# Attention in bursts of three units throughout, and the last output columns stored in small groups from two queues

## The chip, the core and the metric

The kernel runs on one core of one Trainium2 chip. The metric is device time in microseconds (us), the median of several executions. A profile shows one execution; its span (first to last instruction) is some 2 us shorter than the device time. PE is the matrix engine (TensorE), DVE is VectorE, ACT is ScalarE, POOL is GpSimd, SP is the engine that only issues transfers.

## The reference, cut to what matters

```python
# q, k, v: (8 batches, 12 heads, 448, 64); d_model 768, d_ff 2048
scores = (q @ k.T) / sqrt(64)
attn   = max(scores, 0)**2 / 448          # no softmax
x      = attn @ v                         # to (3584, 768)
h      = x @ w_in                         # FFN1
g      = max(h, 0) + alpha * min(h, 0)
out    = g @ w_out                        # FFN2, float32
```

## The kernel before

Four heads form a quad; there are three quads to a batch, 24 in all. One **unit** (n, j) is the scores of quad n for one of seven blocks of rows: four matmuls that each use a quarter of PE's array (64x64), side by side. ACT and DVE turn a unit into squares. "av" is the product of a quad's squares with v, 28 quarter matmuls. FFN1 (`hps`) and FFN2 (`ops`) use the full array, 128x128. The program interleaves them by hand: while PE works on the FFN of batch b, bursts of attention units of batch b + 1 are put in between, so that ACT and DVE have time for them.

```python
def scores(n, j, relu="act", space=sc_ps):
    # 4 matmuls into sc_ps (two buffers in all) or into two of the four mm_ps buffers;
    # relu "act": ACT alone, 896 columns; "both": ACT and DVE one half each;
    # "act2": ACT, in two halves; "dve": DVE alone
...
def burst(n, i):                   # batch 1's attention (quads 3 to 5)
    if i == 0:
        scores(n, 0); squares()
        if (n - 1, 0) in att: attnv(n - 1)
    else:
        for j in (2 * i - 1, 2 * i):          # two units
            scores(n, j, ...); squares()
...
play([(3, 3), o[0], turn(4), o[1], (4, 0), o[2], (4, 1), o[3], ...])   # o[i]: 8 FFN2 matmuls
...
def ffn2(sb, c, hf, half):         # 128 rows x 384 columns, 16 matmuls in two steps
    ...
    nc.vector.tensor_copy(o[:, bass.ts(hf, 384)], ps)
    if hf == 1:
        for u in range(2):         # two stores of 64 x 768 float32, both from SP
            nc.sync.dma_start(out=rows[j], in_=o[64 * u:64 * u + 64])
```

From batch 2's attention on, bursts hold three units already; the first takes its buffers from `mm_ps`, the two others from `sc_ps`.

In the views below, `sc` and `sch` are scores in `sc_ps` and in `mm_ps`, `tps` PE's transposes of q and k, `rl` the relus, `at` the squares, and `neg` and `gT` the two steps of FFN1's activation. In the code, `f[i]` and `o[i]` are pieces of FFN1 and FFN2, `turn(n)` is the transposes of quad n, `feed` is casts, and `g("40", "41", "3a")` is a burst of units (4, 0) and (4, 1) with quad 3's av.

## Time and profile before

| | before |
|---|---|
| device time, median | 401.09 us (400.79 to 401.98, 4 runs) |
| span of the profiled run | 399.3 us |
| PE busy | 387.3 us, 97% |
| DVE, ACT, POOL busy | 65%, 55%, 18% |

I cut every profile into five stages by PE's own work, because single stages repeat far better than whole executions of one kernel, which differ by a us or more: with the same instructions, batch 1 and last FFN (below) agree to 0.02 us in all profiles. The **opening** runs from the start of the span to the first FFN1 matmul behind quad 3's transposes. **Batch 1** goes from there to the end of quad 5's av. The **middle** goes on to the first matmul of the last batch's FFN1 (a block of 96). **Last FFN** ends with the last matmul, and the **end** is what is left of the span. Each border is the start or the end of a piece in the chain of work. Before, these are 37.01, 41.92, 276.55, 38.97 and 4.85 us.

### The profile page before, as it was taken

The page shows a single profiled execution, that of the slowest core. Times are in us where ns is not written, and L with a number is a line of the kernel's source. Part 1 is how long each engine was busy: PE and PEld are TensorE (multiplying, and loading weights), DVE is VectorE, ACT ScalarE, POOL GpSimd, SP SyncE. Part 2 cuts the span into 40 slices and gives each one's busy share as a digit, 9 for nine tenths or more (in the row PEclk, how much of TensorE's full clock was granted, in tenths as well). Part 3 has the DMA queues.
Part 4 walks back from the last instruction along what each step waited for, and adds up shares of the span by engine and source line. Part 5 has one row for each costly group of instructions (what it writes and reads, how often), then busy time and mean ns, then how long its engine had stood idle before and what let it go on. Part 6 is the DMA issues. An engine that isn't in the chain of part 4 may idle for free.

```text
span 399.3 us, 7923 instructions
## 1 busy us (share of the span) xinstructions
PE 387.3 (97%) x3201; PEld 200.8 (50%) x3201; DVE 258.1 (65%) x411; ACT 221.0 (55%) x345; POOL 72.8 (18%) x88
## 2 busy tenths in 40 slices
PE   8788999999999999999999999999999999999995
PEld 5434455444555445544555455554555445555562
DVE  3775767768664877567665777768575776736411
ACT  5785754788544766456544775656464585624200
POOL 6564000022021430033020360033002300000000
PEclk9699999999999999999999999999999999999999
DMA  6999995494098933393097961295058720130033
GB/s 145 189 209 205 203 250 204 116 242 150 21 244 202 252 136 80 86 270 100 2 215 197 250 192 43 64 274 155 2 144 187 200 48 0 41 79 2 0 80 79
DMA packets 64164, 55.44 MB, mean 139 GB/s; under 512 B 35696, under 2 KB 59776, under 8 KB 64128
## 3 DMA queue, kind: packets, MB, share of 16 engines
q1 hardware_dynamic: 53152, 44.98, 43.7%
q0 software_dynamic: 10976, 9.96, 15.6%
q8 instruction: 25, 0.41, 0.4%
q14 instruction: 11, 0.09, 0.1%
HBM read 45.62 MB, written 11.01 MB: 142 GB/s over the span
## 4 chain that ended last, share of the span: by engine, by line
PE 92%; DVE 2%; DMA 2%; ACT 1%; issue 1%; POOL 0%; ACTq 0%
PE ops L247 38%; PE hps L231 35%; PE av L202 7%; PE sc L159 6%; PE sch L159 4%; DMA qe<-in_q_dram 2%; DVE at L184 1%; PE tps L134 1%; DMA qraw<-in_q_dram 1%; PE avh L202 1%; ACT rl L173 0%; DVE gT L239 0%; ACT xT L211 0%; ACT xT L217 0%; POOL ke L103 0%
## 5 line engine op out<-in xcount | busy, mean ns | idle before, releaser
L247 PE MATMUL ops<-w_out_sb,gT 128*128 128x384 bf16 x896 | 153.4, 327 | 0.0
L231 PE MATMUL hps<-xT,w_in_sb 128*128 128x448 bf16 x768 | 151.2, 353 | 1.4 <-ACT xT L211 0.5
L184 DVE TENSOR_TENSOR at<-rl 128x896 bf16<-128x896 bf16 x167 | 111.1, 685 | 19.0 <-ACT rl L173 8.8
L247 PEld LDWEIGHTS <-gT 128*128 128x128 bf16 x896 | 84.1, 98 | 67.2 <-issue 14.7
L231 PEld LDWEIGHTS <-w_in_sb 128*128 128x128 bf16 x768 | 73.1, 98 | 75.7 <-issue 10.2
L239 DVE SCALAR_TENSOR_TENSOR gT<-neg,beta_sb,hps 128x448 bf16<-128x448 f32 x128 | 83.9, 677 | 35.7 <-ACT neg L238 35.1
L173 ACT ACTIVATE rl<-sc 128x896 bf16<-128x896 f32 x109 | 95.8, 927 | 7.7 <-PE sc L159 5.3
L238 ACT ACTIVATE neg<-hps 128x448 f32<-128x448 f32 x128 | 68.4, 553 | 55.0 <-PE hps L231 52.9
L255 DVE COPY osb<-ops 128x384 f32<-128x384 f32 x56 | 31.1, 555 | 54.5 <-PE ops L247 54.5
L109 POOL CAST kb<-kraw 128x896 bf16<-128x896 f32 x16 | 16.2, 1011 | 210.0 <-DMA kraw<-in_k_dram 210.0
L165 ACT ACTIVATE rl<-sch 128x448 bf16<-128x448 f32 x37 | 20.1, 544 | 56.4 <-PE sch L159 56.4
L159 PE MATMUL sc<-qT,kT 64*64 64x448 bf16 x464 | 36.4, 362 | 2.7 <-ACT rl L173 2.2
L202 PE MATMUL av<-at,vb 64*64 64x448 bf16 x616 | 33.1, 350 | 0.0
L166 DVE TENSOR_SCALAR rl<-sch 128x448 bf16<-128x448 f32 x37 | 23.0, 620 | 14.1 <-PE sch L159 14.1
L159 PEld LDWEIGHTS <-kT 64*64 64x64 bf16 x672 | 14.9, 106 | 29.6 <-issue 25.0
L202 PEld LDWEIGHTS <-vb 64*64 64x64 bf16 x672 | 20.3, 110 | 13.2 <-issue 1.4
L169 ACT ACTIVATE rl<-sch 128x448 bf16<-128x448 f32 x30 | 14.6, 544 | 16.9 <-PE sch L159 16.9
L217 ACT ACTIVATE xT<-av 128x896 bf16<-128x896 f32 x21 | 19.4, 922 | 6.8 <-PE av L202 6.7
L159 PE MATMUL sch<-qT,kT 64*64 64x448 bf16 x208 | 20.3, 380 | 0.0
L109 POOL CAST qb<-qraw 128x896 bf16<-128x896 f32 x16 | 18.4, 1151 | 0.0
L109 POOL CAST vb<-vraw 128x896 bf16<-128x896 f32 x16 | 16.8, 1053 | 1.4 <-DMA vraw<-in_v_dram 0.8
L171 DVE TENSOR_SCALAR rl<-sc 128x896 bf16<-128x896 f32 x6 | 6.5, 1084 | 2.9 <-PE sc L159 2.9
(47 smaller groups left out, 72.6 us busy)
## 6 DMA issues: line engine op xcount, KB each, us to landing
out_dram<-osb SPq DMA_DIRECT2D x56, 192.0 KB, 2.8
qraw<-in_q_dram SPq DMA_DIRECT2D x19, 448.0 KB, 4.6
kraw<-in_k_dram SPq DMA_DIRECT2D x19, 448.0 KB, 5.3
vraw<-in_v_dram SPq DMA_DIRECT2D x18, 448.0 KB, 6.3
w_out_sb<-in_moe_w_out_dram POOLq DMA_DIRECT2D x2, 1536.0 KB, 19.8
w_in_sb<-in_moe_w_in_dram POOLq DMA_DIRECT2D x8, 192.0 KB, 8.2
w_in_sb<-in_moe_w_in_dram POOLq DMA_DIRECT2D x4, 384.0 KB, 9.7
vb<-in_v_dram POOLq DMA_DIRECT2D x6, 224.0 KB, 9.9
```

What stands on the lines that cost most here:

```text
L109: eng.tensor_copy(o, i)
L159: nc.tensor.matmul(half[r][64 * c:64 * c + 64, :S], kT[n][64 * r:64 * r + 64, j, c, :], qT[n][64 * r:64 * r + 64, :, c, :], start=True, st ...
L165: nc.scalar.activation(rl[:, 0], half[0][:, :S], ACTF.Relu)
L166: nc.vector.tensor_scalar(rl[:, 1], half[1][:, :S], 0.0, None, ALU.max)
L173: nc.scalar.activation(rl, ps[:, :, :S], ACTF.Relu)
L184: nc.vector.tensor_tensor(a, rl, rl, ALU.mult)
L202: nc.tensor.matmul(half[r][64 * s:64 * s + 64, :S], vb[n][64 * r:64 * r + 64, s, j, :], a[64 * r:64 * r + 64, s], start=(j == 0), stop=(j ...
L231: nc.tensor.matmul(ps, w_in_sb[:, km // 2, km % 2, bass.ts(ff, 128)], xT[b][:, km // 2, km % 2, :], start=(km == 0), stop=(km == KM - 1))
L238: nc.scalar.activation(neg, ps, ACTF.Relu, scale=-1.0)
L239: nc.vector.scalar_tensor_tensor(gT[b // 2][:, ff, (b % 2) * S:(b % 2) * S + S], neg, beta_sb[:, ff:ff + 1], ps, ALU.mult, ALU.add)
L247: nc.tensor.matmul(ps, gT[sb][:, ff, bass.ts(c, 128)], w_out_sb[:, ff, bass.ts(hf, 384)], start=(ff == 0), stop=(ff == KF - 1))
L255: nc.vector.tensor_copy(o[:, bass.ts(hf, 384)], ps)
```

## The change

The intent was to have fewer switches between attention and FFN on PE in batch 1's attention, to relieve ACT there, and to shorten what follows the last matmul.

```diff
-def burst(n, i): ...                       # one, two, two, two units of a quad
+def group(units, how="both"): ...          # up to three units or av; the first of three in mm_ps
 ...
-play([..., (3, 0), f[8], f[9], f[10], (3, 1), f[11], f[12], f[13], (3, 2), f[14], f[15]])
+play([..., f[8], g("30", "31", "32"), f[9], f[10], f[11], f[12],
+      g("33", "34", "35"), f[13], f[14], f[15]])
-play([(3, 3), o[0], turn(4), o[1], (4, 0), o[2], (4, 1), o[3], (4, 2), o[4], (4, 3), o[5], o[6], turn(5), o[7],
-      (5, 0), feed(6, "k"), o[8], (5, 1), feed(6, "q"), o[9], (5, 2), feed(6, "v"), o[10], (5, 3), feed(7, "k", "q"), o[11]])
+play([g("36"), turn(4), o[0], o[1], g("40", "41", "3a"), o[2], o[3], g("42", "43", "44"), o[4], o[5],
+      g("45", "46"), o[6], turn(5), o[7], g("50", "51", "4a"), feed(6, "k", "q"), o[8], o[9],
+      g("52", "53", "54"), feed(6, "v"), o[10], g("55", "56"), feed(7, "k", "q"), o[11]])
 ...
-                to_bf16(n, w, nc.scalar)                              # casts of quads 6 and 7
+                to_bf16(n, w, nc.scalar if n == 6 else nc.vector)
 ...
-        n_in, n_out = ((2, 6) if b % 2 else (3, 5))                  # bursts in FFN1, FFN2
-        if b == 1:
-            n_in += 1
+        n_in, n_out = ((2, 7 if b == 1 else 6) if b % 2 else (3, 5))
 ...
+def ffn2_last(sb, c):                      # the last 128 rows only
+    for w in (384, 256, 128):
+        ... 16 matmuls of w columns, then
+        nc.vector.tensor_copy(o[:, lo:lo + w], ps)
+        for u in range(2):
+            (nc.sync, nc.scalar)[u].dma_start(out=rows[j][:, lo:lo + w], in_=o[64 * u:64 * u + 64, lo:lo + w])
```

Quad 8's casts stay on POOL but are issued as an item of their own in batch 1's FFN1.

More of the change, by code (lines that the diff above doesn't have):

```diff
@@ L261, in ffn2 @@
                 nc.sync.dma_start(out=rows[j], in_=o[64 * u:64 * u + 64])
+    def ffn2_last(sb, c):
+        o = o_sb[(sb, c)] = o_pool.tile([128, d_model], F32, tag="o", name="osb")
+        lo = 0
+        for w in (384, 256, 128):
+            ps = mm_ps.tile([128, 384], F32, tag="mm", name="ops")[:, :w]
+            for ff in range(KF):
+                nc.tensor.matmul(ps, gT[sb][:, ff, bass.ts(c, 128)], w_out_sb[:, ff, lo:lo + w],
+                                 start=(ff == 0), stop=(ff == KF - 1))
+            nc.vector.tensor_copy(o[:, lo:lo + w], ps)
+            for u in range(2):
+                blk = 2 * c + u
+                b, j = 2 * sb + blk // NJ, blk % NJ
+                rows = out[b * S:(b + 1) * S].rearrange("(pp j) d -> j pp d", j=NJ)
+                (nc.sync, nc.scalar)[u].dma_start(out=rows[j][:, lo:lo + w], in_=o[64 * u:64 * u + 64, lo:lo + w])
+            lo += w
     def steps(b, what):
@@ L270, with group, f, spread @@
     NQ = len(quads)
-    relu_on_dve = {(n, j) for n in range(NG + 1, 2 * NG) for j in (1, 3, 5)}
-    def burst(n, i):
-        if i == 0:
-            if n < NQ:
-                scores(n, 0)
-                squares()
-            if (n - 1, 0) in att:
-                attnv(n - 1)
-        elif n < NQ:
-            for j in (2 * i - 1, 2 * i):
-                scores(n, j, "dve" if (n, j) in relu_on_dve else "act")
-                squares()
-    def spread(seq, bursts, share=0.92):
+    def group(units, how="both"):
+        def f():
+            order = sorted(units, key=lambda u: u[1] == "av")
+            for i, (n, j) in enumerate(order):
+                if j == "av":
+                    attnv(n)
+                elif i == 0 and len(order) == 3:
+                    scores(n, j, how, mm_ps)
+                else:
+                    scores(n, j)
+            squares()
+            for n, j in order:
+                if n < n_pe:
+                    continue
+                if j == 0:
+                    if n + 2 < NQ:
+                        load(n + 2)
+                    if n + 1 < NQ:
+                        transpose(n + 1, "k")
+                        transpose(n + 1, "q")
+                if j == 4 and n > 2 * NG and n + 2 < NQ:
+                    for w in "kqv":
+                        to_bf16(n + 2, w, nc.gpsimd)
+        return f
+    def spread(seq, items, share=0.92):
         total = sum(x[0] for x in seq) * share
@@ L289, in spread @@
         for cost, fn in seq:
-            while n < len(bursts) and done >= total * n / len(bursts):
-                for f in bursts[n] if isinstance(bursts[n], list) else [bursts[n]]:
-                    f() if callable(f) else burst(*f)
+            while n < len(items) and done >= total * n / len(items):
+                items[n]()
                 n += 1
@@ L295, in spread @@
             done += cost
-        assert n == len(bursts)
+        assert n == len(items)
     warm_w = singles.tile([128, 128], BF16)
@@ L377, in play, with g @@
         for x in seq:
-            if isinstance(x, list):
-                play(x)
-            elif callable(x):
-                x()
-            else:
-                burst(*x)
+            x()
+    def g(*units):
+        return group([(int(u[0]), "av" if u[1:] == "a" else int(u[1:])) for u in units])
     for ff in range(4):
@@ L388 @@
     f = [fn for _, fn in steps(0, "in")]
-    play([f[4], f[5], turn(3), f[6], f[7], (3, 0), f[8], f[9], f[10], (3, 1), f[11], f[12], f[13], (3, 2), f[14], f[15]])
+    play([f[4], f[5], turn(3), f[6], f[7], f[8], g("30", "31", "32"), f[9], f[10], f[11], f[12],
+          g("33", "34", "35"), f[13], f[14], f[15]])
     load_bf16(5)
@@ L412 @@
     stream.append((NQ - 1, "av"))
-    parts, todo_u = [], list(stream)
-    while todo_u:
-        m = 2 if not parts else 3
-        parts.append(todo_u[:m])
-        del todo_u[:m]
-    def group(units, phase):
-        def f():
-            units_ = sorted(units, key=lambda u: u[1] == "av")
-            for i, (n, j) in enumerate(units_):
-                if j == "av":
-                    attnv(n)
-                elif i == 0 and len(units_) == 3:
-                    scores(n, j, "act2" if phase == "in" else "both", mm_ps)
-                else:
-                    scores(n, j)
-            squares()
-            for n, j in units_:
-                if j == 0:
-                    if n + 2 < NQ:
-                        load(n + 2)
-                    if n + 1 < NQ:
-                        transpose(n + 1, "k")
-                        transpose(n + 1, "q")
-                if j == 4 and n + 2 < NQ:
-                    for w in "kqv":
-                        to_bf16(n + 2, w, nc.gpsimd)
-        return f
+    parts = [stream[:2]] + [stream[i:i + 3] for i in range(2, len(stream), 3)]
     count = 0
     for b in range(1, B - 1):
-        n_in, n_out = ((2, 6) if b % 2 else (3, 5))
-        if b == 1:
-            n_in += 1
+        n_in, n_out = ((2, 7 if b == 1 else 6) if b % 2 else (3, 5))
         if b == B - 2:
@@ L450 @@
         mlp = steps(b, "in")
-        spread(mlp[3:] if b == 1 else mlp, [group(x, "in") for x in parts[count:count + n_in]], 0.95)
+        bursts = [group(x, "act2") for x in parts[count:count + n_in]]
+        if b == 1:
+            bursts.append(lambda: [to_bf16(2 * NG + 2, w, nc.gpsimd) for w in "kqv"])
+        spread(mlp[3:] if b == 1 else mlp, bursts, 0.95)
         count += n_in
-        spread(steps(b, "out"), [group(x, "out") for x in parts[count:count + n_out]], 0.92)
+        spread(steps(b, "out"), [group(x) for x in parts[count:count + n_out]], 0.92)
         count += n_out
-    for _, fn in steps(B - 1, "in") + steps(B - 1, "out"):
+    for _, fn in steps(B - 1, "in") + steps(B - 1, "out")[:-4]:
         fn()
+    ffn2_last(B // 2 - 1, NJ - 1)
 _INS = ['q', 'k', 'v', 'moe_w_in', 'moe_w_out', 'moe_alpha']
```

## The prediction

> **What bounds the kernel now.** I read the page's busy shares first, then the chain that ended last, then the list of what TensorE (PE) waited for, then the chain in order of time through batch 1's attention (36 to 79 us) and the timeline of the last 5 us.
>
> ```profile
> PE 387.3 (97%) x3201; PEld 200.8 (50%) x3201; DVE 258.1 (65%) x411; ACT 221.0 (55%) x345; POOL 72.8 (18%) x88
> PE 92%; DVE 2%; DMA 2%; ACT 1%; issue 1%; POOL 0%; ACTq 0%
> ```
>
> PE is busy for 97% of the 399.3 us span and carries 92% of the chain. VectorE at 65% and ScalarE at 55% are far from a bound on average. The list of waits of PE, asked for from 50 us to the end, holds one line:
>
> ```profile
> PE hps L231 <- ACT xT L217: 0.2, 1, 0.2
> ```
>
> So after the opening nothing keeps PE waiting for long. The time can fall only if PE has less to do, or if the 4.8 us after its last matmul get shorter. The stretch that the change rewrites looks so in the chain in order of time (start, duration, what):
>
> ```profile
> 57.37 0.50 PE sc L159 x8
> 57.87 1.41 PE ops L247 x8
> 59.28 0.50 PE sc L159 x8
> 59.78 1.41 PE ops L247 x8
> 61.19 0.31 PE sc L159 x4
> 61.54 0.38 PE sc L159 x4
> 61.92 2.71 PE ops L247 x16
> 64.63 0.90 PE tps L134 x28
> ...
> 104.01 0.31 PE sch L159 x4
> 104.32 0.38 PE sc L159 x8
> 104.70 2.71 PE ops L247 x16
> ```
>
> Attention matmuls here are 64x64 pieces, four side by side; FFN matmuls are 128x128. Eight FFN2 matmuls take 1.41 us and sixteen take 2.71, so one costs (2.71 - 1.41) / 8 = 0.1625 us and each stretch begins with 1.41 - 8 x 0.1625 = 0.11 us extra. One unit of scores (4 matmuls) takes 0.31 us alone, two take 0.50 and three 0.31 + 0.38 = 0.69: 0.19 us for a unit and 0.12 us extra at the start. **An excursion from the full array to small tiles and back costs 0.12 + 0.11 = 0.23 us, whether it carries one unit or three.** From 104 us on bursts already hold three units; in batch 1's attention they hold two. There is also a hole at 61.50 to 61.54 plus a slow first piece: the two units of that burst take 0.73 us instead of 0.50. The burst at 73.80 does the same.
>
> The end of the kernel, from the timeline:
>
> ```profile
> 394.48 0.56 DVE L255 COPY osb<-ops 128x384 f32<-128x384 f32 x1 [2.04 <-PE ops L247]
> 395.06 1.11 SPq L261 DMA_DIRECT2D out_dram<-osb  x2
> ```
>
> After the last matmul (394.45) come one copy of 384 columns, then two stores of 192 KB, issued one after the other from one queue. The second starts 0.55 us after the first. The issue list gives 2.8 us from issue to landing, and the span ends at 399.3.
>
> **What the Trainium skill says.** TensorEngine Tiling, Key Properties: changing the tiling mode, and not only the tile, drains the array. The trace agrees: the extra 0.11 to 0.12 us appears only where small and full tiles meet, and not between scores and attention-times-v, which share a mode (28 of those take 1.32 us right behind scores). TensorE: Matmul & The Clock Gate, Back-to-back issue gap: in a stream of weight load and matmul pairs, 128 columns take about 81 ns, more than the 56 ns of the columns alone. No such stream of full tiles runs in the kernel before, so this prices the new last group. DMA: Bandwidth & Descriptors, Anatomy of one DMA: about 2.0 us fixed, plus bytes at 436 GB/s. For a 192 KB store that gives 2.45 us; the trace has 2.8, with 2.6 the least. The same page, Issuing engines are not separate DMA queues: starting transfers from two engines saves only the time to initiate them, which is the 0.55 us here.
>
> **The change part by part.**
>
> *Batch 1's bursts.* From the instruction order of both kernels, PE's excursions from the start of the first transposes (36.1 us) to the end of quad 5's attention-times-v (78.95) fall from 16 to 12: quad 3's scores 0 to 5 go in two bursts instead of three; quads 4 and 5 lose one burst each; and score 6 of quad 3 stands directly before quad 4's transposes. There a switch from 64x64 to 128x64 tiles remains, about 0.12 us. Saved: 4 x 0.23 - 0.12 = 0.80 us. To check the model: content of this stretch is 96 FFN2 matmuls x 0.1625 + 68 FFN1 x 0.189 + 21 units x 0.1875 + 3 x 1.312 for attention-times-v + 84 transposes x 0.028 = 38.7 us. Adding 16 x 0.23 = 3.7 gives 42.35, and the trace has 42.84. The 0.49 us left over are the two slow bursts (2 x 0.23).
>
> *Waits in these bursts.* Those two slow bursts had to wait for the two score buffers, because the bursts stood only eight FFN2 matmuls (1.41 us) apart while ScalarE or VectorE needs 0.93 or 1.08 us per relu. In the new order most bursts are 16 matmuls apart, and one of three units takes a buffer from the other pool. One pair stays eight apart: 2, 3, 4 of quad 5, then 5, 6. Counting ScalarE from the burst's start: half a relu ready at 0.3, done at 0.85, then two whole relus to 1.77 and 2.7. PE comes to unit 6 at 0.69 + 1.41 + 0.31 = 2.4. So one wait of about 0.3 us is left: 0.46 - 0.3, say 0.2 saved.
>
> *VectorE and ScalarE there.* ScalarE loses quad 7's three casts (0.93 us each) and VectorE gains them, about 0.6 us each, estimated from its 0.394 us for 448 columns and 0.416 for 512. VectorE also takes half a relu (0.62 us) per burst of three but sheds six whole relus (1.08 each). I walked the FFN1 stretch with one burst per four steps: VectorE's gT results free their matmul buffers some 0.2 us or more before PE wants them. Tight, but no wait: 0.
>
> *The burst moved from FFN1 to FFN2 in batch 1.* The count of excursions stays nine. FFN2 gets seven bursts 16 matmuls apart, spacing that later batches already run without a wait. PE waits in neither phase now: 0. Quad 8's casts stay on GpSimd with the same order there: 0.
>
> *The last columns.* PE runs 16 x 0.1625 = 2.6, 16 x 0.109 = 1.75 for 256 columns, and for 128 columns 16 x 0.081 = 1.3 by the skill or 0.9 by columns alone; I take 1.1. The sum 5.45 against 5.2 is +0.25. The copy falls from 0.56 to about 0.29 us (an estimate from 0.165 for 16 columns and 0.555 for 384). The second store no longer queues: -0.55. Each store is 32 KB instead of 192: -0.4 by the skill's rate, and I take -0.5 because its formula came out low. Sum: 0.25 - 0.27 - 0.55 - 0.5 = -1.07.
>
> **Total:** -0.80 - 0.2 - 1.07 = -2.1 us on 401.23, which is **399.2 us** (0.5% faster).
>
> **The rivals.**
> *A new wait replaces the switches.* With three units and six VectorE passes behind one burst, PE could stall on the score or matmul buffers in FFN1 of batch 0. For it: my margin there is 0.2 us. Against it: from 104 us on the same bursts run between 16 FFN2 matmuls without a wait. If two or three bursts each stall 0.3 us, the gain of the first part is gone: about 400.2.
> *VectorE becomes the bound locally.* The casts of quad 7 stand before the copy that frees a matmul buffer and before FFN1's first gT. If these come late, PE waits at the start of batch 1's FFN1: +0.5 to 1, about 400. Against it: three more matmul buffers are used before that one returns, some 4 us.
> *The end does not shorten.* Completion may not depend on size, ScalarE's first store may start late, and the 128-column group may be held by its weight loads (98 ns each as recorded, 1.6 us). Then the end gives only about -0.2 and the total is 400.0.
> *More than expected.* If weight loads hide and small stores land in about 2 us, the total is near 398.6.
>
> **Range and chances.** These sizes add to a spread of about 0.8 us, and the three runs before spread from 400.79 to 401.98, so the range is 398.2 to 400.6. Two per cent would be 8 us; nothing here can give or cost that unless a buffer wait cascades. Faster 0.01, within 2% 0.98, slower 0.01.
>
> **What would show it.** In the chain, batch 1's stretch should be about 41.8 us instead of 42.84, with bursts of 0.31 + 0.38 us, and 16 FFN2 matmuls at 2.71. After the last matmul, copy, stores and end should take about 3.5 us instead of 4.85, and the 128-column group 0.9 to 1.3 us. I am wrong if waits of PE on ScalarE or VectorE above 0.5 us in sum appear between 36 and 100 us, if that stretch keeps 42.8 us, or if the last stores land as late after issue as before.

## The result, and the profile after

The changed kernel takes **398.52 us** (397.68 to 399.12, 4 runs) against 401.09. The ratio is 0.9931, 95% interval 0.9907 to 0.9955. Ratios here are the mean time of one kernel's fast runs over that of the other's of the same rounds, so not quite the ratio of the medians. The gain is 2.6 us by the medians, and the interval allows 1.8 to 3.7.

The page's busy shares, and what PE waited for from 36 us to the end, from the profile after:

```profile
PE 386.4 (97%) x3217; PEld 202.3 (51%) x3217; DVE 257.0 (65%) x416; ACT 220.8 (56%) x347; POOL 73.6 (19%) x88
PE hps L231 <- DVE gT L239: 0.2, 1, 0.2
PE hps L231 <- ACT xT L217: 0.2, 1, 0.2
```

PE is still the bound. There are 16 more matmuls (the last columns in three groups instead of two), and yet 0.9 us less of busy time.

The chain of work after, in order of time, in batch 1's stretch (start, duration, what):

```profile
57.82 0.31 PE sch L159 x4
58.13 0.38 PE sc L159 x8
58.51 2.71 PE ops L247 x16
...
69.97 0.37 PE sch L159 x4
...
70.76 1.73 ACT rl L173 x2
72.49 0.04 issue
72.53 0.38 PE sc L159 x4
72.91 1.41 PE ops L247 x8
```

The bursts now have the form that later batches had before: 0.31 + 0.38 us for three units, 2.71 us for sixteen FFN2 matmuls, nothing in between. The lower lines show the one place where the chain leaves PE: unit 6 of quad 5 waits for ACT's relus, because its burst stands only eight FFN2 matmuls behind the last. This wait, some 0.35 us, isn't in the list of PE's waits above: a list without an entry doesn't show that PE waited for nothing, so I look at the chain too.

The end after, from the timeline, and the last lines of the list of transfers (KB each, us from issue to landing):

```profile
391.16 2.84 SPq L277 DMA_DIRECT2D out_dram<-osb  x3
391.16 3.00 ACTq L277 DMA_DIRECT2D out_dram<-osb  x3
392.32 0.42 DVE L272 COPY osb<-ops 128x256 f32<-128x256 f32 x1 [1.19 <-PE ops L270]
393.21 0.29 DVE L272 COPY osb<-ops 128x128 f32<-128x128 f32 x1 [0.47 <-PE ops L270]
out_dram<-osb SPq DMA_DIRECT2D x1, 96.0 KB, 2.1
out_dram<-osb ACTq DMA_DIRECT2D x1, 96.0 KB, 2.4
out_dram<-osb SPq DMA_DIRECT2D x1, 32.0 KB, 1.8
out_dram<-osb ACTq DMA_DIRECT2D x1, 32.0 KB, 2.0
```

The last copy takes 0.29 us, and the last stores land 1.8 and 2.0 us after issue; the 192 KB stores of before took 2.8. The stages of all kernels follow. They were timed in several sets on different chips, with the kernel before in each set (medians of 401.05 to 401.73 us), so kernels are compared by the ratio and not by the median:

| kernel | median us | ratio to before | opening | batch 1 | middle | last FFN | end |
|---|---|---|---|---|---|---|---|
| before | 401.09 | | 37.01 | 41.92 | 276.55 | 38.97 | 4.85 |
| changed | 398.52 | 0.9931 | 36.30 | 41.01 | 276.87 | 39.01 | 3.51 |
| bursts only | 399.97 | 0.9974 | 36.41 | 41.00 | 276.83 | 38.97 | 4.89 |
| end only | 399.24 | 0.9958 | 35.98 | 41.93 | 276.52 | 39.01 | 3.46 |
| one queue | 399.68 | 0.9971 | 35.40 | 41.00 | 276.97 | 39.01 | 4.62 |
| halves, two queues | 398.80 | 0.9946 | 36.01 | 41.00 | 277.51 | 38.97 | 4.01 |
| quad 7's casts on ACT | 398.71 | 0.9927 | 37.47 | 41.00 | 276.50 | 39.01 | 3.52 |
| burst back in FFN1 | 399.51 | 0.9944 | 36.05 | 41.00 | 277.30 | 39.01 | 3.94 |
| bursts of two later | 403.45 | 1.0040 | 37.13 | 41.01 | 282.13 | 39.01 | 3.42 |
| bursts of four | 407.31 | 1.0153 | 36.73 | 40.66 | 289.43 | 39.01 | 3.47 |
| later casts off POOL | 402.15 | 1.0017 | 37.11 | 41.00 | 279.82 | 39.01 | 3.86 |
| other pool | 397.98 | 0.9925 | 36.67 | 40.66 | 276.41 | 39.01 | 3.45 |
| before, second look | 400.97 | | 36.28 | 41.92 | 276.80 | 38.97 | 4.93 |
| changed, second look | 397.34 | | 35.72 | 41.00 | 276.33 | 39.01 | 3.44 |

Before to changed, the two spans differ by 2.6 us: opening -0.71, batch 1 -0.91, middle +0.32, last FFN +0.04, end -1.34. Two of these, batch 1 and the end, are where the change acts. The same new end took 3.42 to 3.52 us in seven profiles of the table, but 3.86 and 3.94 in two (in the second of these the 32 KB stores landed 2.2 and 2.3 us after issue; the first is not explained). So a difference of less than some 0.5 us between two ends of the table, one profile each, is not certain. The experiments ask whether the two gains are independent and what each consists of, and whether the other differences belong to the change.

### The profile page after: what moved, and what is told of

Read it like the earlier page. It is cut to its first block, busy times and chain, and to the rows that moved or that the text cites. A ratio compares the mean times of both kernels' runs of the same rounds, so it can differ in the third digit from the quotient of the medians.

```text
span 396.7 us, 7988 instructions
## 1 busy us (share of the span) xinstructions
PE 386.4 (97%) x3217; PEld 202.3 (51%) x3217; DVE 257.0 (65%) x416; ACT 220.8 (56%) x347; POOL 73.6 (19%) x88
## 4 chain that ended last, share of the span: by engine, by line
PE 90%; DVE 4%; ACT 3%; issue 1%; ACTq 0%
PE ops L247 36%; PE hps L231 34%; PE av L202 7%; PE sc L159 5%; PE sch L159 4%; DVE at L184 3%; ACT rl L173 2%; PE warm L336 1%; PE ops L270 1%; PE tps L134 1%; DVE rl L166 1%; DVE gT L239 0%; ACT rl L169 0%; DVE qT L109 0%; ACT xT L211 0%
## 5 line engine op out<-in xcount | busy, mean ns | idle before, releaser
L247 PE MATMUL ops<-w_out_sb,gT 128*128 128x384 bf16 x864 | 147.9, 327 | 0.0
L247 PEld LDWEIGHTS <-gT 128*128 128x128 bf16 x864 | 81.1, 98 | 64.9 <-issue 14.2
L255 DVE COPY osb<-ops 128x384 f32<-128x384 f32 x54 | 30.0, 555 | 52.3 <-PE ops L247 52.3
L165 ACT ACTIVATE rl<-sch 128x448 bf16<-128x448 f32 x44 | 24.0, 545 | 59.3 <-PE sch L159 59.3
L159 PE MATMUL sc<-qT,kT 64*64 64x448 bf16 x440 | 33.9, 354 | 4.1 <-ACT rl L173 1.6
L166 DVE TENSOR_SCALAR rl<-sch 128x448 bf16<-128x448 f32 x44 | 27.3, 620 | 15.4 <-PE sch L159 15.4
L169 ACT ACTIVATE rl<-sch 128x448 bf16<-128x448 f32 x28 | 13.7, 543 | 16.9 <-PE sch L159 16.9
L159 PE MATMUL sch<-qT,kT 64*64 64x448 bf16 x232 | 22.4, 374 | 0.0
L109 POOL CAST vb<-vraw 128x896 bf16<-128x896 f32 x16 | 17.9, 1116 | 1.1 <-DMA vraw<-in_v_dram 0.7
L144 POOL DMA_DIRECT2D w_in_sb<-in_moe_w_in_dram x12 | 7.5, 630 | 4.4 <-DMA w_in_sb<-in_moe_w_in_dram 1.9
```

Source lines behind the costliest of these rows:

```text
L109: eng.tensor_copy(o, i)
L159: nc.tensor.matmul(half[r][64 * c:64 * c + 64, :S], kT[n][64 * r:64 * r + 64, j, c, :], qT[n][64 * r:64 * r + 64, :, c, :], start=True, st ...
L165: nc.scalar.activation(rl[:, 0], half[0][:, :S], ACTF.Relu)
L166: nc.vector.tensor_scalar(rl[:, 1], half[1][:, :S], 0.0, None, ALU.max)
L247: nc.tensor.matmul(ps, gT[sb][:, ff, bass.ts(c, 128)], w_out_sb[:, ff, bass.ts(hf, 384)], start=(ff == 0), stop=(ff == KF - 1))
```

## The experiments

### Each half of the change alone

The first kernel is the changed one with the old end, the second is the kernel before with the new end.

```diff
 bursts only:
-    for _, fn in steps(B - 1, "in") + steps(B - 1, "out")[:-4]: fn()
-    ffn2_last(B // 2 - 1, NJ - 1)
+    for _, fn in steps(B - 1, "in") + steps(B - 1, "out"): fn()
 end only: the reverse of this, in the kernel before
```

> The changed kernel with the old end (two halves of 384 columns, two stores of 192 KB from one queue). If the two parts are independent, as I hold, batch 1's stretch takes 41.9 us as in the changed kernel (42.84 before), and from the last matmul to the end of the span 4.85 us as before; the time is about 0.95 us below before (ratio about 0.9976). If the gain came from the end alone, the stretch is 42.8 us and the time equals before. The first 36 us should vary by some tenths of a us between runs of all kernels, as the instructions there are the same in all.

> The kernel before with only the new end (last columns in groups of 384, 256 and 128, two queues). By my theory batch 1's stretch stays 42.8 us, the last 48 matmuls take 5.25 us against 5.2, and the end after the last matmul falls from 4.85 to 3.5 us; time about 1.3 us below before (ratio about 0.9968). If the new end gained only by something that the bursts made possible, the end stays near 4.85 us.

Bursts only: batch 1 took 41.00 us and the end 4.89; ratio 0.9974 (0.9951 to 0.9997). End only: batch 1 41.93, last FFN 39.01 and the end 3.46; ratio 0.9958 (0.9934 to 0.9981). (The stretches of 42.84 and 41.9 us in my expectations begin at the start of quad 3's transposes; the table's begin behind them, 0.90 us later.) The halves act each in its own stage and add up: 0.92 us and 1.35 us net of the 0.04 us in the last matmuls. They are two independent changes.

### What shortens the end: queue, copy or bytes

Two kernels, both the changed one but for one line each.

```diff
 one queue:
-            (nc.sync, nc.scalar)[u].dma_start(...)
+            nc.sync.dma_start(...)
 halves, two queues:
-    for w in (384, 256, 128):
+    for w in (384, 384):
```

> The changed kernel, but all stores of the last columns go from the one queue as before, so that the last store is issued some 0.5 us after the one before it. If half of the gain at the end is the second queue, as I reckoned (0.55 us of 1.32), the end after the last matmul is 4.0 to 4.1 us instead of 3.5. If only the size of the last copy and stores counts, it stays 3.5 us.

> The changed kernel with two groups of 384 columns in place of 384, 256 and 128, still stored from two queues, each group by itself (96 KB each). The last copy is 0.56 us again instead of 0.29, and the last stores carry 96 instead of 32 KB. By my sums: 0.27 us more for the copy and some 0.2 us for the bytes, so the end after the last matmul is about 4.0 us instead of 3.5. If bytes don't count at all it is 3.8; if only the queue counted, 3.5. The last matmuls take 5.2 us instead of 5.25.

With halves from two queues the end took 4.01 us, as I reckoned. With one queue it took 4.62 us, where I had expected 4.0 to 4.1: a miss. The timeline of this kernel's last stores, all on SP:

```profile
390.36 4.00 SPq L277 DMA_DIRECT2D out_dram<-osb  x6
391.51 0.42 DVE L272 COPY osb<-ops 128x256 f32<-128x256 f32 x1 [1.19 <-PE ops L270]
392.41 0.29 DVE L272 COPY osb<-ops 128x128 f32<-128x128 f32 x1 [0.47 <-PE ops L270]
```

The last copy ends at 392.70. At that time SP is still issuing the second store of the 256-column group: four stores of 0.55 to 0.59 us each follow one another from 391.97, and the last one starts at 393.8, 1.1 us behind the copy. I had counted one store in the way, and there are two. **Small groups alone are worth only 4.85 - 4.62 = 0.23 us; the second queue is what lets them pay.** Going the other way, halves from two queues give 0.84 us, and the smaller groups the remaining 0.50, of which 0.27 us is the shorter copy. The 0.84 is not the queue alone, because each half is now stored by itself and the last stores carry 96 KB instead of 192; two queues with stores of 192 KB were not tried.

### Where quad 7's casts run, and the moved burst

```diff
 casts on ACT:
-                to_bf16(n, w, nc.scalar if n == 6 else nc.vector)
+                to_bf16(n, w, nc.scalar)
 burst back in FFN1:
-        n_in, n_out = ((2, 7 if b == 1 else 6) if b % 2 else (3, 5))
+        n_in, n_out = ((3 if b == 1 else 2, 6) if b % 2 else (3, 5))
         # quad 8's casts right behind the second burst
```

> The changed kernel with quad 7's three casts on ScalarE again instead of VectorE. My theory: ScalarE then has 2 casts (1.86 us) behind the last relus of quad 5 and one before FFN1's first results, and VectorE some 1.85 us less; no more than 0.3 us of new waits, so batch 1's stretch stays 41.0 to 41.3 us (from the end of the first transposes) and the time within 0.3 us of the changed kernel. Rival: the move of these casts is what makes the three-unit bursts pay; then PE waits for ScalarE there and the stretch grows by 0.5 us or more.

> The changed kernel with the moved burst put back: three bursts in batch 1's FFN1 and six in FFN2, quad 8's casts right behind the second burst, as before. The move costs or gives nothing in the count of excursions. The stretch from quad 5's attention-times-v to the last FFN1 (276.5 us with the old bursts, 276.8 to 277.5 in all runs with the new) is what I look at: if the move shifts later loads and casts so that VectorE's squares collide with GpSimd's casts in FFN1 of batch 3, it falls back to 276.5 us here; if the surplus comes from elsewhere, it stays at 276.8 or more. Time within 0.5 us of the changed kernel in either case.

With the casts back on ACT, batch 1 took the same 41.00 us and the ratio was 0.9927: their move is worth nothing here. With the burst back in FFN1 the middle took 277.30 us, and not the 276.5 that a cause in the move would have given. But kernels with the move took anything from 276.33 to 277.51 us there, so this one profile can't decide it. The time (ratio 0.9944, 0.9908 to 0.9980) isn't told apart from the changed kernel's. Neither part of the change earns anything measurable.

### Is an excursion really 0.23 us?

The bursts of batches 1 to 6 were cut from three units to two, so that PE leaves the full array 24 times more, with all else alike.

```diff
-    parts = [stream[:2]] + [stream[i:i + 3] for i in range(2, len(stream), 3)]
+    parts = [stream[:2], stream[2:3]] + [stream[i:i + 2] for i in range(3, len(stream), 2)]
     # the first of two units in mm_ps too; bursts (3, 9) and (5, 7), in batch 1 (3, 11)
```

> The changed kernel with the bursts of batches 1 to 6 cut to two units: PE leaves the full array 92 times instead of 68. At 0.23 us for an excursion, the stretch after batch 1's attention grows by 24 x 0.23 = 5.5 us, and the time by the same, to about 404 us, even above the kernel before. If the drain were hidden (rival: the extra time at the edges is only how the profile models matmul ends), the time stays near 398.5 us. Waits for buffers could add to it; they would show as waits of PE.

The middle grew to 282.13 us. The eight other profiles of kernels with bursts of three throughout and their casts on GpSimd took 276.33 to 277.51 us there, 276.84 on average, so 24 excursions cost 5.3 us (4.6 to 5.8 from the ends of that range), which is 0.22 us each (0.19 to 0.24). The whole kernel became slower than before (ratio 1.0040, 1.0002 to 1.0077); against the changed kernel's 0.9931 that is some 4.4 us, give or take almost 2. The chain of this kernel shows it:

```profile
106.27 0.31 PE sch L159 x4
106.59 0.19 PE sc L159 x4
106.78 1.41 PE ops L247 x8
```

Each excursion has its 0.12 us at the first unit and its 0.11 us at the first FFN2 matmul, and no wait for data is seen in these pieces. The list from 37 us on has only 0.2 us for xT, and in the middle the chain leaves PE at one place (231 to 236 us). The rival, that this time is only how the profile draws the ends of matmuls, falls with the device time.

### Fewer excursions still, and the wait that is left

The kernel with bursts of four puts up to four units into FFN2's bursts, between finished column groups; it also takes the first buffer of quad 5's last burst from the other pool. The last kernel has this second edit alone.

```diff
 other pool (in both):
-                elif i == 0 and len(order) == 3:
+                elif i == 0 and (len(order) == 3 or other):
-          g("52", "53", "54"), feed(6, "v"), o[10], g("55", "56"), ...
+          g("52", "53", "54"), feed(6, "v"), o[10], g("55", "56", other=True), ...
 bursts of four: FFN2's bursts of sizes 4, 4, 4, 3 (even b) and 4, 4, 4, 4, 2 (odd b);
     the third unit of four in mm_ps too
```

> A try at something better: FFN2's bursts hold up to four units, placed only between finished column groups so that the fourth unit can use the second pair of the other pool's buffers (63 excursions instead of 68), and the burst with units 5 and 6 of quad 5 takes its first buffer from the other pool, so that the one wait left in batch 1's stretch (0.36 us) should go. Expected: 5 x 0.23 + 0.36 = 1.5 us less than the changed kernel, about 397.0 us. Rival: VectorE, with 3.7 us of work behind a burst of four, frees the buffers too late, PE waits, and nothing is won or some is lost.

> The changed kernel, only that the burst with units 5 and 6 of quad 5 takes its first buffer from the other pool (as in the run with bursts of four, whose batch 1 stretch was 40.66 us). Expected: the last wait in batch 1's stretch is gone, 40.65 us instead of 41.0, all else as in the changed kernel, time 0.35 us below it (about 398.2 us, ratio to before about 0.992). If the wait moves on to quad 5's attention-times-v or to FFN1, the stretch stays 41.0.

Bursts of four failed: 407.31 us, ratio 1.0153 (1.0097 to 1.0210). The profiled execution, 411.07 us, was the slowest of the four; the others took 406.39 to 407.34. Its chain at a burst of four, and the copy of the FFN2 columns finished just before:

```profile
102.77 0.31 PE sch L159 x4
103.08 0.19 PE sc L159 x4
103.27 0.52 PE sch L159 x4
102.80 0.56 DVE L255 COPY osb<-ops 128x384 f32<-128x384 f32 x1 [1.95 <-PE ops L247]
```

The rival I had written down is there, and it is the larger loss: buffers come free too late. The third unit takes 0.52 us instead of 0.19, as it has to wait for the `mm_ps` buffer that VectorE's copy empties at 103.36; this is seen in 13 bursts, 4.3 us in sum, and stands in no list of waits. In six others, at the start of FFN2, PE waits for ACT's relus of the first unit: the list has 2.3 us for it, and these bursts take about 0.74 us more than their content each, 4.4 us in sum. That is 8.7 us, against 5 x 0.23 = 1.15 saved. The profiled execution has another loss:

```profile
162.37 7.52 DMA qT<-qb
170.02 0.38 PE sch L159 x4
170.40 0.19 PE sc L159 x4
170.59 2.22 PE av L202 x28
172.81 3.45 PE ops L247 x16
```

PE sat idle from 167.8 to 170.0 for the transposed q of the next quad. Transposes go through the same SP queue as the stores and loads and were issued too late. Behind that idle time the granted clock was 0.66 from 170 to 175 us, and the av took 2.22 instead of 1.32 us and sixteen FFN2 matmuls 3.45 instead of 2.71. At 217 us PE waited again for a transposed q, 0.6 us, and the clock stayed at 1.00. All this is some 4.5 us, and since the other three executions were about 4 us faster, they may not have had it. The reckoning of excursions is not refuted, but this way of saving them costs more than it saves.

The other pool alone did what was expected. The chain in batch 1's stretch:

```profile
72.43 0.31 PE sch L159 x4
72.74 0.19 PE sc L159 x4
72.93 1.41 PE ops L247 x8
```

The wait is gone and batch 1 took 40.66 us. The kernel took 397.98 us, ratio 0.9925 (0.9903 to 0.9946). That is the lowest ratio of all, though several are not told apart from it; by the stage it is 0.35 us better than the changed kernel, but in the total the intervals overlap, so the whole-kernel gain over the changed one is not shown.

### What makes the middle vary

The middle took 276.3 to 277.5 us in kernels whose bursts of three are the same there. In the profile after, a look at VectorE and GpSimd between 171.2 and 174 us:

```profile
171.27 2.61 DVE L184 TENSOR_TENSOR at<-rl 128x896 bf16<-128x896 bf16 x2 [0.18 <-ACT rl L173]
171.20 0.93 POOL L109 CAST kb<-kraw 128x896 bf16<-128x896 f32 x1 [26.11 <-DMA kraw<-in_k_dram]
172.07 1.33 POOL L109 CAST qb<-qraw 128x896 bf16<-128x896 f32 x1
173.34 1.32 POOL L109 CAST vb<-vraw 128x896 bf16<-128x896 f32 x1
```

Two squares take 2.61 us where two usually take 1.24, while GpSimd casts; the last two casts take 1.33 and 1.32 us instead of 0.93. Behind them gT is late and PE waits, 0.2 us by its list. The Trainium skill says in SBUF — State Buffer, Who interferes with whom, that a VectorE instruction with two inputs in this memory contends with a GpSimd instruction that reads it, and that the second to issue is blocked. So all casts from quad 9 on were taken off GpSimd.

```diff
-                if j == 4 and n > 2 * NG and n + 2 < NQ:
-                    for w in "kqv":
-                        to_bf16(n + 2, w, nc.gpsimd)
+                if j == 6 and n > 2 * NG and n + 2 < NQ:
+                    for w in "kq":
+                        to_bf16(n + 2, w, nc.scalar)
+                if j == 1 and n - 1 > 2 * NG and n + 1 < NQ:
+                    to_bf16(n + 1, "v", nc.scalar)
```

> The changed kernel with the casts of quads 9 to 23 taken from GpSimd and given to ScalarE, later in the quad. All runs so far show one to three places in FFN1 of batches 2 to 6 where two squares on VectorE take 2.5 to 2.7 us instead of 1.25 while GpSimd casts, and PE waits 0.2 to 0.5 us for a gT behind them; the stretch after batch 1's attention then takes 276.5 to 277.5 us. If the casts on GpSimd slow VectorE, the mean square in that stretch falls from 0.70 us to 0.62, these places go and the stretch is 276.3 us or less. Rival: the slow squares come from transfers into the on-chip memory and stay. It can also happen that ScalarE, which gets 15 x 2.8 = 42 us more, runs late in FFN1 and PE waits for it instead; then the mean square still tells the cause.

The squares' group of the middle in this kernel, and PE's wait:

```profile
L184 DVE TENSOR_TENSOR at<-rl 128x896 bf16<-128x896 bf16 x126 | 77.3, 625 | 20.8 <-ACT rl L173 8.3 <-ACT rl L169 5.5 <-ACT rl L165 3.9
PE hps L231 <- DVE gT L239: 3.0, 5, 0.6
```

The mean square fell from 700 to 625 ns, and no slow pair is left: the cause is the casts on GpSimd, as the page says. But ACT, with 255.5 us of work instead of 220.8, now runs its casts ahead of FFN1's first half (neg). PE waits 0.6 us for gT in five places, and the middle takes 279.82 us. The cure is worse than the harm.

### Second looks

> The kernel before, unchanged, for a second profile. If the opening and the middle vary by chance, batch 1's stretch is again 41.9 us and the end 4.85 us, while the opening ends anywhere between 35.4 and 37.5 us and the stretch after batch 1's attention takes 276.5 to 277.5 us. If the old bursts are free of the slow squares by design, that stretch is 276.5 again.

> The changed kernel, unchanged, for a second profile: batch 1's stretch 41.0 us, the last 48 matmuls 5.25 us, the end 3.5 us again; the opening anywhere between 35.4 and 37.5 us, and the stretch after batch 1's attention 276.5 to 277.5 us, with the slow squares at other places than 171 and 181 us if they are chance.

Both came out as expected, but for the middle of the changed kernel, which was a little below the range told. Batch 1 and the end repeat to within 0.1 us (41.92 and 4.93; 41.00 and 3.44). The opening and the middle don't. With the old bursts the middle was 276.55, 276.52 and 276.80; with the new ones 276.33 to 277.51. Slow squares are in all these eleven kernels and looks, those with the old bursts too: the mean square of the middle is 696 to 715 ns in each. What differs is whether PE waits for a gT behind them. PE's list has no such wait in the five with a middle of 276.33 to 276.55 us, 0.2 to 0.3 us in the four with 276.80 to 276.97, and 0.5 to 0.7 us in the two with 277.30 and 277.51. The ranges of old and new bursts overlap, and whether the new bursts lose some tenths here on average stays open. The opening, whose instructions are the same in all kernels, ended at 36.4 us on average in the three profiles with the old bursts and at 36.5 in the eleven with the new. In one of them (end only) its last transposes waited 1.04 us for a load of q. So the 0.71 us that it gave between the first two profiles counts as chance.

## Why the prediction was right

The prediction was 399.2 us, within 398.2 to 400.6, and the measured median is 398.52, with the place and the size of both gains as told. Point by point:

- **Excursions and waits in batch 1** (-0.80 and -0.2): measured -0.91 by the table. In the prediction's own borders the stretch took 41.91 us, against the 41.8 told. The unit of 0.23 us is confirmed by the bursts of two (0.22). The wait left over measured 0.35 us (41.01 less 40.66 when it was removed), and I had said about 0.3, so the waits saved were about 0.1 us rather than 0.2. With that wait removed too, batch 1 is 1.26 us below before, the 0.80 of the excursions and the 0.46 of both slow bursts.
- **The tight FFN1 stretch, quad 7's casts, the moved burst** (0 each): right as far as is seen. The chain shows no wait of PE in batch 1 but that one. The casts on VectorE took 0.62 us each, and moving them back left batch 1 at 41.00 us; moving the burst back left the middle within its spread.
- **The last matmuls** (+0.25): the one term clearly mis-sized. It measured +0.04, because the 128-column group ran at 56 ns for a matmul instead of the 69 I took between the skill's 81 and the columns alone: its copy starts 0.89 us after that of the 256-column group, and 0.89 / 16 = 0.056 us. The weight loads added nothing. The rival "the end does not shorten" rested partly on this, and it fell.
- **The copy** (-0.27): right, 0.56 to 0.29 us.
- **Second queue and bytes** (-0.55 and -0.5): right in sum, as the end fell by 1.34 us, of which 1.07 are left after the copy. The split is not a plain sum: the queue is worth 1.11 us with small groups, as these make more stores, and was not measured alone with the old ones. The term for the bytes is not confirmed on its own. I took 0.4 to 0.5 us from a formula that the skill gives for transfers that GpSimd issues, while these stores go from SP and ACT. In the trace 32 KB land 1.8 (SP) and 2.0 us (ACT) after issue and 192 KB from SP after 2.8 (the median of 56, the least 2.6), so the step is rather 0.6 to 1.0 us. By 0.8 the end should have fallen by 1.6 us; that the sum is right is in part luck.
- **The total**: batch 1, last FFN and end give -0.91 + 0.04 - 1.34 = -2.2 us, and I had said -2.1. The measured 2.6 (1.8 to 3.7) contains this; the 0.4 us between is no larger than the chance in the opening and the middle.

## What to carry to other kernels

When a bound engine is 97% busy, look for time that it spends on changing its mode of work: take short and long stretches from the chain, and solve for the cost per piece and the cost per start. Merge the pieces as long as the buffers and the transfers behind them keep up; here three units were right, and with four PE lost more to buffers that were not yet free than it saved. At the end of a kernel, cut the last piece small only together with a second queue to issue its stores, or the stores queue up behind each other.

## What the Trainium skill lacked or had wrong

- TensorE: Matmul & The Clock Gate, Back-to-back issue gap: about 81 ns for a matmul of 128 columns in a stream with weight loads. Here sixteen of them, each with its own load, took 0.89 us, 56 ns each, which is the page's figure for a matmul by itself.
- TensorEngine Tiling, Key Properties: the drain at a change of mode has no figure. Here full array to 64x64 and back costs 0.12 + 0.11 us; 24 more such excursions cost 5.3 us (4.6 to 5.8).
- DMA: Bandwidth & Descriptors, Anatomy of one DMA: the sum of 2.0 us and bytes at 436 GB/s is given for transfers that GpSimd issues, and the page has none for stores issued by SP or ACT. For these it is too flat: it would give 2.1 and 2.45 us for 32 and 192 KB (estimates from the page's figures), and SP's stores took 1.8 and 2.8.
- The same page, Issuing engines are not separate DMA queues: it calls the time saved "usually small relative to the DMA itself". Here it was 1.1 us of a 4.6 us end (one profile each), where six stores queued up behind each other. No page says that stores issued by ACT land later than SP's (2.0 against 1.8 us at 32 KB, 2.4 against 2.1 at 96 KB).
- SBUF — State Buffer, Who interferes with whom: right in kind, without a figure for two-input instructions. Two squares beside casts took 2.61 us instead of 1.24, and a cast 1.33 instead of 0.93.
- TensorE: Matmul & The Clock Gate, Why this matters for your kernels: idle gaps of more than about 3 us are said to bring the lower clock. Here, once, a gap of 2.3 us was followed by a granted clock of 0.66 over 5 us.
